# Three regions of SBUF in place of two: where output weights, streams and input weights of the second mixture lie modulo 256 bytes

## The chip, the core and the metric

One core of one Trainium2 chip runs the whole program. The time is device microseconds of that core for one execution. The kernel before takes 1418.29 us (median of three runs, 1417.86 to 1418.48). All data is 32-bit; matrix products run with operands of type fp32r, and to keep precision each product is made of three: a number is split into a high and a low part, and high times high, high times low and low times high are added in PSUM.

## The reference, cut to what matters

```python
def reference(**kw):
    attn = _attn_ref(x, state)               # B, H, S+Ns, D = 8, 8, 544, 64
    x = attn.transpose(0, 2, 1, 3).reshape(4352, 512)
    x = (x @ w_a) * (x @ w_b) @ w_out        # first mixture,  512 -> 1536 -> 512
    h = x @ w_in                             # second mixture, 512 -> 2048
    return (h - tanh(h)) @ w_out2            #                 2048 -> 512
```

Tokens come in nine blocks: blocks 0 to 7 have 512 tokens each (one batch of the attention), block 8 the 256 tokens that the 32 state rows of all batches make.

## The kernel before, in words

**First mixture.** For each block and each of 12 slices f of the hidden width, `AB` (L576) makes two products into PSUM tiles `pab`, multiplies them on VectorE and splits the result into a tile `ph`; `X1` (L602) multiplies `ph` with the slice's output weights `wo` into four accumulators `acc`. In blocks 0 to 7 the weights of `AB` are the small tiles `mx` and the stream (the moving operand) is `hl`, 512 columns wide. In block 8 the weights are `wh` and `wl`, the high and low part of the slice's input weights made in block 1 by `ab_split` (L194), the stream is `x0s`, and every matmul has 256 columns.

**Second mixture.** It runs in 72 slots, eight for each block. A slot of blocks 0 to 7 (`pair_slot`, L755) computes two slices of h by seven half-sized products, `part` (L677): six matmuls of 256 columns each with a piece of the input weights (`wh0`, `wh1` from `wh_load`, L265) as weights and one of the tiles B11 to T4 as stream, into PSUM tiles `px`, `py`, `pz`. The elementwise work of h - tanh(h) (`act_ut` to `g_lo`, L688 to L720) leaves a tile `g`, high and low, and `O` (L722) multiplies `g` as stream, 512 columns, with the output weights `wo2` (`wo_load`, L276) into `acc`. So a slot has 42 matmuls of 256 columns and 24 of 512. The eight slots of block 8 (`plain_slot`, L839) have 24 and 24 matmuls, all of 256 columns.

Every matmul has a weight load of its own, 128 by 128, and the queue of TensorE brings the load of the next matmul beside the stream of the one that runs. The order of work is written out by hand; PE, ACT and DVE each take their instructions in that order, and POOL's queue issues `wo_load` and `wh_load`.

**Where tiles lie.** SBUF tiles come from pools, and the pools are laid one behind the other in the order in which they are opened. Each tile takes a multiple of 256 bytes in a partition, with the exception of the constants (`consts`, 64 bytes, in the pool `step`) and of some at the very end. So all tiles of the pools ahead of `step` start at one residue modulo 256, called 0 here, and all tiles behind it at 64. Slices inside a tile begin at multiples of 256 bytes, so a matmul's operand has the residue of its tile. In the kernel before, the pool `front` has residue 0: the tiles `w` with an even number (`w_tile`, L102) and x6, x7. The pools `wp`, `xp` and `sp` have residue 64: `w` with an odd number, all `v`, x0 to x5, and the slots q, r and m. That puts

- the second mixture's streams B11 to T4 at 0 (`XT`, L632), its input weights `wh0`, `wh1` at 64 (tiles `v`), its output weights `wo2` at 64 (`OPL`, L274) and its stream `g` at 64 (`g_hi`, L713);
- of the first mixture `hl`, `mx`, `ph`, `wo` and `x0s` all at 64; in block 8 the weights `wh` of f = 0 to 7, 10 and 11 at 64, of f = 8 and 9 at 0 (x6, x7), and `wl` at 0, but for f = 0, where it is in q2 at 64.

What follows writes the distance as the stream's residue less the weights'. It is 0 for `O`, `X1` and `AB` of blocks 0 to 7, and -64 for `part`.

Of the kernel before, what the change touches and what calls it, by code (L numbers as in the profile page):

```python
# [29 lines left out]
class Slots:  # L30


    def __init__(self, pool, names):
        self.pool, self.names, self.at = pool, names, {}

    def get(self, shape, dtype, name, among=None):
        among = among or self.names
        key = tuple(among)
        i = self.at.get(key, 0)
        self.at[key] = i + 1  # L40
        return self.pool.tile(shape, dtype, tag=among[i % len(among)], name=name)


@with_exitstack
def fused_kernel(ctx: ExitStack, tc, xT, xn, stp, stq, wA, wB, outT, outS):
# [6 lines left out]
    wp = ctx.enter_context(tc.tile_pool(name="wp", bufs=1))  # L52
    xp = ctx.enter_context(tc.tile_pool(name="xp", bufs=1))
    sp = ctx.enter_context(tc.tile_pool(name="sp", bufs=1))
# [5 lines left out]
    ident = cp.tile([128, 128], F32, tag="ident", name="ident")  # L60
    consts = step.tile([128, 16], F32, tag="consts", name="consts")
    make_identity(nc, ident)
    nc.vector.memset(consts[:, 0:1], PA)
    nc.vector.memset(consts[:, 1:2], -T2)

# [24 lines left out]
    ab = Slots(abp, ["p2", "p3"])  # L90
    big = Slots(sp, [f"q{i}" for i in range(6)])
    small = Slots(sp, [f"r{i}" for i in range(8)])
    mix = Slots(sp, [f"m{i}" for i in range(4)])
    Q, R = big.names, small.names
# [10 lines left out]
    def v_tile(i, shape, dtype, name):  # L105
        return wp.tile(shape, dtype, tag=f"v{i}", name=name)

    def x_tile(i, shape, name, dtype=F32R):
        return (xp if i < 6 else front).tile(shape, dtype, tag=f"x{i}", name=name)

# [162 lines left out]
    WP = {}  # L273
    OPL = [("x", 0)] + [("w", i) for i in range(1, 24, 2)] + [("x", i) for i in (4, 5, 2)]  # L274

    def wo_load(i):  # L276

        f = i // 2 + FP * (i % 2)
        kind, at = OPL[i]
        WB[f] = (w_tile(at, [128, 2, 512], F32R, f"wo2_{f}") if kind == "w"  # L280
                 else x_tile(at, [128, 2, 512], f"wo2_{f}"))
        nc.gpsimd.dma_start(flat(WB[f]), wod[f])
# [293 lines left out]
    def AB(blk, f, bg=None, after=None):  # L576
        n = 512 if blk < NB else 256
        a = None
        for s in range(2):
            pt = ab.get([128, 512], F32, "pab")  # L580
            if blk < NB:
                m = MM[blk, f]
                for G in range(2):
                    product(pt, (m(0, G, s), m(1, G, s)), HL[blk][G], slice(0, n), G == 0, G == 1)
            else:
                for k in range(KT):
                    product(pt, [w[:, s, k, :] for w in WH[f]], X0S[k], slice(0, n), k == 0, k == KT - 1)
            if s == 0:
                a = small.get([128, 512], F32, "ac", AC) if blk < NB else big.get([128, 512], F32, "ac", RAW)
                nc.scalar.copy(a[:, :n], pt[:, :n])  # L590
        if bg:
            bg()
        at_v = nc.vector.tensor_tensor(a[:, :n], a[:, :n], pt[:, :n], ALU.mult)  # L593
        ph = big.get([128, 2, 512], F32R, "ph", PHS)
        at_s = nc.scalar.copy(ph[:, 0, :n], a[:, :n])
        nc.vector.tensor_tensor(ph[:, 1, :n], a[:, :n], ph[:, 0, :n].bitcast(F32), ALU.subtract)
        PH[blk, f] = ph
        if after:
            with tc.issue_after(at_v.ins), tc.issue_after(at_s.ins):
                after()  # L600
# [30 lines left out]
    slots = [(blk, j) for blk in border for j in range(FP)]  # L631
    XT = [[("w", 2 * i) for i in range(7)], [("w", 2 * i) for i in range(7, 12)] + [("x", 6), ("x", 7)]]  # L632

# [3 lines left out]
    def xr_load(blk, parts=(0, 1)):  # L637
        n = 512 if blk < NB else 256
        for i in parts:
            t = x_tile(1, [128, 2, 512], "x1s", F32) if i else big.get([128, 2, 512], F32, "x1r", XIN)  # L640
            for m in range(2):
                nc.sync.dma_start(t[:, m, :n], x1d[blk][2 * i + m])
            RAWX.setdefault(blk, []).append(t)
        XB[blk] = {}
# [53 lines left out]
    def act_k(s, g):  # L698
        u, t, y, k = EW[s, g]
        nc.scalar.activation(k, u, AF.Relu, bias=consts[:, 1:2], scale=1.0)  # L700

# [11 lines left out]
    def g_hi(s, g):  # L713
        GG[s, g] = big.get([128, 2, 512], F32R, "g", Q[2:3] + mix.names[0:2] + Q[0:2])
        nc.scalar.copy(GG[s, g][:, 0, : width(s)], EW[s, g][2])  # L715
# [273 lines left out]
    for f in range(FA):  # L989
        stages = {4: (0,), 5: (1, 2), 6: (3, 4), 7: (5, 6)}.get(f, ())  # L990
        AB(NB, f, after=lambda: [x_stage(0, i) for i in stages])
        if f == 0:
            wo_load(0)
        if f in (3, 7):
# [4 lines left out]
        if f in (9, 10):  # L999
            next(slot)  # L1000
        if f:
            wo_load(f)
        if f in (1, 3):
            xr_load(0, (f // 2,))
    xr_load(1)
    wh_load(2, slots[2][1])
    for i in range(FA + 1, FB):
        wo_load(i)

    last = len(slots) - 1  # L1010
    for s, (blk, j) in enumerate(slots):
# [4 lines left out]
        if blk < NB:  # L1016
            for i, _ in enumerate(pair_slot(s)):
                if s == 1 and i == 0:
                    X1(NB, FA - 1)
                    wo_load(FA)  # L1020
        else:
# [56 lines left out]
```

## Time and profile before

| what | value |
|---|---|
| median of three runs | 1418.29 us |
| the profiled execution | 1418.56 us |
| its span, first to last instruction | 1416.8 us |
| TensorE busy | 1393.3 us, 98% of the span |
| weight loads busy (they overlap the matmuls) | 1187.5 us |
| VectorE busy | 1124.3 us |
| ScalarE busy | 899.1 us |
| granted clock of TensorE | full in all 40 slices |

The page comes from one execution. A matmul's own duration is longer than the step from one matmul to the next, since they are pipelined: the duration of a group along the chain of waits, divided by its matmuls, is the step. The span has three parts: attention and the start of the first mixture up to about 140 us, the first mixture up to 710 us (its block 8 from 648 us), the second mixture behind that, with block 8 from 1360 us.

### The profile page before, as it was taken

How to read it: one execution, taken by the hardware profiler on the slowest of the kernel's cores; microseconds unless marked ns; L12 is line 12 of the kernel's file. 1: busy time of each engine (PE TensorE's matmuls, PEld its weight loads, DVE VectorE, ACT ScalarE, POOL GpSimd, SP SyncE). 2: the span in 40 equal slices, each digit the busy share in tenths (PEclk: the TensorE clock that was granted, in tenths of full speed). 3: DMA queues.
4: the chain of work that ended last, by engine and by line, in shares of the span. 5: the costliest groups of instructions: out<-in, count | busy, mean ns of one | idle time of the engine just before them, and what ended most of it. 6: DMA issues, size and time to landing. Idle time of an engine off the chain costs nothing.

```text
span 1416.8 us, 23918 instructions
## 1 busy us (share of the span) xinstructions
PE 1393.3 (98%) x8928; PEld 1187.5 (84%) x8928; DVE 1124.3 (79%) x1972; ACT 899.1 (63%) x1740; POOL 207.4 (15%) x390
## 2 busy tenths in 40 slices
PE   6999999999999999999999999999999999999998
PEld 3666767888888878889989999999998999999998
DVE  7986656887544879772498999989899898998887
ACT  5765445565444556552477777777777877778675
POOL 0000002333111333321211110111101111011110
PEclk9999999999999999999999999999999999999999
DMA  9614348685546686855876667566665756667544
GB/s 376 259 56 138 128 136 249 212 270 176 160 127 178 178 264 225 251 174 173 259 241 207 202 191 231 179 209 196 208 213 180 230 175 213 207 191 217 164 149 128
DMA packets 103780, 280.49 MB, mean 198 GB/s; under 512 B 15216, under 2 KB 44400, under 8 KB 93936
## 3 DMA queue, kind: packets, MB, share of 16 engines
q0 software_dynamic: 41472, 178.28, 40.8%
q1 hardware_dynamic: 62192, 100.68, 21.9%
q8 instruction: 70, 1.15, 0.3%
q14 instruction: 46, 0.38, 0.1%
HBM read 216.53 MB, written 62.39 MB: 197 GB/s over the span
## 4 chain that ended last, share of the span: by engine, by line
PE 66%; DVE 22%; ACT 8%; issue 3%; DMA 1%; DVEq 0%; SPq 0%; ACTq 0%
PE acc L458 30%; PE pab L458 20%; PE px L680 6%; DVE u L705 3%; DVE y L704 3%; DVE y L709 3%; DVE t L710 3%; PE pz L680 3%; PE mq L546 2%; DVE y L711 2%; ACT g L715 2%; ACT u L691 2%; ACT y L696 2%; PE ph L823 2%; DVE g L720 2%
## 5 line engine op out<-in xcount | busy, mean ns | idle before, releaser
L458 PE MATMUL acc<-g,wo 128*128 128x512 f32 (+1 forms) x1728 | 425.3, 378 | 0.1
L458 PEld LDWEIGHTS acc<-g,wo 128*128 128x128 f32 x1728 | 289.8, 188 | 36.0 <-DVE g L720 0.3
L458 PE MATMUL acc<-ph,wo 128*128 128x512 f32 (+1 forms) x1296 | 305.7, 381 | 0.0
L458 PE MATMUL pab<-hl,mx 128*128 128x512 f32 x1152 | 291.2, 397 | 0.3 <-ACT ac L590 0.2
L458 PEld LDWEIGHTS acc<-ph,wo 128*128 128x128 f32 x1296 | 230.3, 188 | 50.5 <-issue 6.6
L458 PEld LDWEIGHTS pab<-hl,mx 128*128 128x128 f32 x1152 | 209.8, 188 | 52.7 <-issue 4.2
L593 DVE TENSOR_TENSOR ac<-ac,pab 128x512 f32<-128x512 f32 (+1 forms) x108 | 70.6, 654 | 126.0 <-PE pab L458 124.2
L269 POOL DMA_DIRECT2D wh<-whd x144 | 77.6, 539 | 632.9 <-PE pz L680 584.0
L715 ACT CAST g<-y 128x512 fp32r<-128x512 f32 (+1 forms) x144 | 86.2, 598 | 98.6 <-DVE y L711 97.3
L568 POOL DMA_DIRECT2D ml<-md x144 | 75.6, 527 | 408.8 <-DVE mx L574 235.5
L680 PEld LDWEIGHTS px<-T,wh 128*128 128x128 f32 x768 | 105.5, 189 | 13.3 <-ACT snap L782 0.9
L704 DVE SCALAR_TENSOR_TENSOR y<-y,u 128x512 f32<-128x512 f32 (+1 forms) x144 | 94.8, 658 | 27.4 <-ACT y L696 27.2
L590 ACT COPY ac<-pab 128x512 f32<-128x512 f32 (+1 forms) x108 | 60.5, 560 | 83.3 <-PE pab L458 83.0
L680 PE MATMUL px<-T,wh 128*128 128x256 f32 x768 | 111.6, 281 | 0.1
L680 PE MATMUL pz<-T,wh 128*128 128x256 f32 x768 | 111.3, 281 | 0.0
L680 PE MATMUL px<-B,wh 128*128 128x256 f32 x768 | 111.3, 281 | 0.0
L680 PEld LDWEIGHTS px<-B,wh 128*128 128x128 f32 x768 | 104.1, 189 | 5.0 <-ACT snap L791 0.2
L680 PEld LDWEIGHTS pz<-T,wh 128*128 128x128 f32 x768 | 104.1, 189 | 5.0 <-DVE h L794 0.2
L711 DVE COPY_PREDICATED y<-k,t 128x512 f32<-128x512 int32 (+1 forms) x144 | 104.3, 725 | 2.8
L705 DVE SCALAR_TENSOR_TENSOR u<-t,u 128x512 f32<-128x512 f32 (+1 forms) x144 | 94.4, 655 | 9.3 <-ACT k L700 1.0
L720 DVE TENSOR_TENSOR g<-y,g 128x512 fp32r<-128x512 f32 (+1 forms) x144 | 94.4, 656 | 8.2 <-ACT g L715 8.2
L700 ACT ACTIVATE k<-u,consts 128x512 f32<-128x512 f32 (+1 forms) x144 | 99.7, 692 | 0.0
(161 smaller groups left out, 2062.6 us busy)
## 6 DMA issues: line engine op xcount, KB each, us to landing
wh<-whd POOLq DMA_DIRECT2D x64, 1024.0 KB, 5.3
wh<-whd POOLq DMA_DIRECT2D x72, 768.0 KB, 4.7
ml<-md POOLq DMA_DIRECT2D x144, 128.0 KB, 2.9
raw<-in_wB SPq DMA_DIRECT2D x32, 512.0 KB, 4.4
whd<-hlb POOLq DMA_DIRECT2D x64, 256.0 KB, 3.1
rawab<-in_wA SPq DMA_DIRECT2D x12, 1024.0 KB, 9.7
md<-mst SPq DMA_DIRECT2D x48, 256.0 KB, 2.6
x1d<-ev SPq DMA_DIRECT2D x32, 256.0 KB, 3.1
```

Source lines behind the costliest of these rows:

```text
L269: nc.gpsimd.dma_start(t.rearrange("p a h c -> p a (h c)"), whd[j][:, a:b])
L458: nc.tensor.matmul(dst[:, cols], w[a], x[:, c, cols], start=first and i == 0, stop=last and i == 2)
L568: nc.gpsimd.dma_start(t[64 * G : 64 * G + 64, :], src[G, b])
L590: nc.scalar.copy(a[:, :n], pt[:, :n])
L593: at_v = nc.vector.tensor_tensor(a[:, :n], a[:, :n], pt[:, :n], ALU.mult)
L680: nc.tensor.matmul(dst, WP[s, piece][:, a, block(k)], XB[slots[s][0]][x][:, c, k, :], start=first and k == 0 and i == 0, stop=last and k = ...
L700: nc.scalar.activation(k, u, AF.Relu, bias=consts[:, 1:2], scale=1.0)
L704: nc.vector.scalar_tensor_tensor(y, y, PK, u, ALU.add, ALU.mult)
L705: nc.vector.scalar_tensor_tensor(u, t, C3, u, ALU.mult, ALU.mult)
L711: nc.vector.copy_predicated(y, k.bitcast(I32), t)
L715: nc.scalar.copy(GG[s, g][:, 0, : width(s)], EW[s, g][2])
L720: nc.vector.tensor_tensor(gt[:, 1, :n], EW.pop((s, g))[2], gt[:, 0, :n].bitcast(F32), ALU.subtract)
```

## The change

A second pool of 64 bytes (`rise`, with the tile `const2`) stands behind `wp`, so there are three regions: `cp` and `front` at residue 0, `wp` at 64, and the new pool `vp` with `sp` at 128. Tiles move as follows.

- The second mixture's output weights `wo2` go to residue 0: q2 (now in `front`), the even `w` from 0 to 20, x6, x7, x4, x5 (x4 and x5 now in `front`).
- All streams go to 64: B11 to T4 to x0 to x3 and the odd `w` from 1 to 19; `g` to m0, m1, q0, q1 and w21; `hl`, `x0s` and `ph` of blocks 0 to 7 stay at 64, `ph` of block 8 goes to q4 and q5, now at 0.
- The input weights `wh0`, `wh1` (tiles `v`, now in `vp`) go to 128, and with them `wh` of f = 0 to 7 in the first mixture's block 8, while `wh` of f = 10 and 11 and `wl` of f = 0 go to 0. The elementwise tiles r, m2, m3 and q3 go to 128 too; the raw tiles q4, q5 to 0.
- `wo_load(f)` is issued right behind `AB` of block 8, ahead of `X1`, since its tile is now the `wl` that `AB` has just read; `wo_load` of 11 to 15 stands behind `wh_load(2)`; none is left in slot 1. `ac` of block 8 comes from r3 and r4, and half of the raw x1 (`x1s`) lands in w22.

No matmul, elementwise instruction or byte of DMA is added or removed.

```diff
-    def __init__(self, pool, names):
+    def __init__(self, pool, names, homes={}):
...
+        tag = among[i % len(among)]
+        return self.homes.get(tag, self.pool).tile(shape, dtype, tag=tag, name=name)
...
     wp = ctx.enter_context(tc.tile_pool(name="wp", bufs=1))
-    xp = ctx.enter_context(tc.tile_pool(name="xp", bufs=1))
+    rise = ctx.enter_context(tc.tile_pool(name="rise", bufs=1))
+    vp = ctx.enter_context(tc.tile_pool(name="vp", bufs=1))
     sp = ctx.enter_context(tc.tile_pool(name="sp", bufs=1))
...
+    const2 = rise.tile([128, 16], F32, tag="const2", name="const2")
...
-    nc.vector.memset(consts[:, 1:2], -T2)
+    nc.vector.memset(const2[:, 0:1], -T2)
...
-    big = Slots(sp, [f"q{i}" for i in range(6)])
+    big = Slots(sp, [f"q{i}" for i in range(6)], {**{n: front for n in ("q2", "q4", "q5")}, **{n: wp for n in ("q0", "q1", "m0", "m1", "w21")}})
...
-    mix = Slots(sp, [f"m{i}" for i in range(4)])
+    mix = Slots(sp, [f"m{i}" for i in range(4)], {"m0": wp, "m1": wp})
...
     def v_tile(i, shape, dtype, name):
-        return wp.tile(shape, dtype, tag=f"v{i}", name=name)
+        return vp.tile(shape, dtype, tag=f"v{i}", name=name)
...
-        return (xp if i < 6 else front).tile(shape, dtype, tag=f"x{i}", name=name)
+        return (wp if i < 4 else front).tile(shape, dtype, tag=f"x{i}", name=name)
...
-    OPL = [("x", 0)] + [("w", i) for i in range(1, 24, 2)] + [("x", i) for i in (4, 5, 2)]
+    OPL = [None] + [("w", i) for i in range(0, 22, 2)] + [("x", i) for i in (6, 7, 4, 5)]
...
-        ph = big.get([128, 2, 512], F32R, "ph", PHS)
+        ph = big.get([128, 2, 512], F32R, "ph", PHS if blk < NB else RAW)
...
-    XT = [[("w", 2 * i) for i in range(7)], [("w", 2 * i) for i in range(7, 12)] + [("x", 6), ("x", 7)]]
+    XT = [[("x", 2 * b), ("x", 2 * b + 1)] + [("w", 10 * b + 2 * i + 1) for i in range(5)] for b in range(2)]
...
-            t = x_tile(1, [128, 2, 512], "x1s", F32) if i else big.get([128, 2, 512], F32, "x1r", XIN)
+            t = w_tile(22, [128, 2, 512], F32, "x1s") if i else big.get([128, 2, 512], F32, "x1r", XIN)
...
-        GG[s, g] = big.get([128, 2, 512], F32R, "g", Q[2:3] + mix.names[0:2] + Q[0:2])
+        GG[s, g] = big.get([128, 2, 512], F32R, "g", MX + PHS + ["w21"])
...
         AB(NB, f, after=lambda: [x_stage(0, i) for i in stages])
-        if f == 0:
-            wo_load(0)
+        wo_load(f)
...
-        if f:
-            wo_load(f)
...
-    for i in range(FA + 1, FB):
+    for i in range(FA, FB):
         wo_load(i)
...
-                    wo_load(FA)
```

## Rows read from the trace of the kernel before

**Rows 1.** The page's parts 1, 2 and 5: busy time and share; granted clock; weight loads.

```profile
span 1416.8 us, 23918 instructions
...
PE 1393.3 (98%) x8928; PEld 1187.5 (84%) x8928; DVE 1124.3 (79%) x1972; ACT 899.1 (63%) x1740; POOL 207.4 (15%) x390
...
PEclk9999999999999999999999999999999999999999
...
L458 PEld LDWEIGHTS acc<-g,wo 128*128 128x128 f32 x1728 | 289.8, 188 | 36.0 <-DVE g L720 0.3
```

**Rows 2.** Busy time by stage in the second mixture, sum of six stretches of 100 us.

```profile
core 0: us, PE busy (x) PEld busy (x) DVE busy (x) ACT busy (x) POOL busy (x), PEclk, DMA share, GB/s
...
sum 600.00, PE 599.94 PEld 542.27 DVE 548.13 ACT 452.33 POOL 61.96; mean PE 99.99 PEld 90.38 DVE 91.35 ACT 75.39 POOL 10.33
```

**Rows 3.** Chain of waits, second mixture at 1097 us: start, duration, engine, line, count.

```profile
1097.06 0.68 PE acc L458 x3
1097.74 0.71 PE pz L680 x6
1098.45 1.36 PE acc L458 x6
```

**Rows 4.** Groups by shape, PE: count, busy time, mean ns of one, idle time.

```profile
L458 PE MATMUL acc<-g,wo 128*128 128x512 f32 x1536 | 400.1, 389 | 0.0
...
L680 PE MATMUL px<-T,wh 128*128 128x256 f32 x768 | 111.6, 281 | 0.1
```

**Rows 5.** Chain of waits, first mixture's block 8 and the change to the second.

```profile
645.41 2.72 PE acc L458 x12
648.13 2.87 PE pab L458 x24
...
653.75 2.83 PE pab L458 x24
656.58 1.44 PE acc L458 x12
...
683.61 2.72 PE pab L458 x24
...
690.50 0.71 PE py L680 x6
...
694.04 0.68 PE pz L680 x6
...
710.39 0.70 PE acc L458 x3
```

**Rows 6.** Groups by line in 414.24 to 414.26 us, PE alone.

```profile
L458 PE MATMUL acc<-ph,wo 128*128 128x512 f32 x2 | 0.6, 388 | 0.0
```

**Rows 7.** Timeline around these two matmuls: start, duration, engine, line, operation.

```profile
413.79 0.84 PE L458 MATMUL acc<-ph,wo 128*128 128x512 f32 x3
...
414.02 0.19 PEld L458 LDWEIGHTS acc<-ph,wo 128*128 128x128 f32 x1
414.56 0.21 PEld L406 LDWEIGHTS pr<-xnt,E2T 128*32 128x32 f32 x12 [0.35 <-issue]
```

**Rows 8.** Chain of waits, second mixture's block 8.

```profile
1372.16 1.41 PE ph L823 x12
...
1375.01 1.38 PE ph L823 x12
1376.39 1.42 PE acc L458 x12
```

**Rows 9.** Groups by shape, ACT and DVE: operations between tiles of different residues.

```profile
L715 ACT CAST g<-y 128x512 fp32r<-128x512 f32 x128 | 79.7, 622 | 95.7 <-DVE y L711 95.2
...
L649 ACT CAST B<-x1s 128x512 fp32r<-128x512 f32 x17 | 10.5, 624 | 0.0
```

**Rows 10.** Waits in 720 to 1340 us: total, times, longest.

```profile
DVE h L807 <- PE pz L680: 17.3, 33, 0.6
```

More of the change, by code (lines that the diff above doesn't have):

```diff
@@ L30 @@
 class Slots:
-    def __init__(self, pool, names):
-        self.pool, self.names, self.at = pool, names, {}
+    def __init__(self, pool, names, homes={}):
+        self.pool, self.names, self.homes, self.at = pool, names, homes, {}
     def get(self, shape, dtype, name, among=None):
@@ L40, in get @@
         self.at[key] = i + 1
-        return self.pool.tile(shape, dtype, tag=among[i % len(among)], name=name)
+        tag = among[i % len(among)]
+        return self.homes.get(tag, self.pool).tile(shape, dtype, tag=tag, name=name)
 @with_exitstack
@@ L273, in fused_kernel @@
     WP = {}
-    OPL = [("x", 0)] + [("w", i) for i in range(1, 24, 2)] + [("x", i) for i in (4, 5, 2)]
+    OPL = [None] + [("w", i) for i in range(0, 22, 2)] + [("x", i) for i in (6, 7, 4, 5)]
     def wo_load(i):
         f = i // 2 + FP * (i % 2)
-        kind, at = OPL[i]
-        WB[f] = (w_tile(at, [128, 2, 512], F32R, f"wo2_{f}") if kind == "w"
-                 else x_tile(at, [128, 2, 512], f"wo2_{f}"))
+        if i == 0:
+            WB[f] = big.get([128, 2, 512], F32R, "wo2_0", LO0)
+        else:
+            kind, at = OPL[i]
+            WB[f] = (w_tile(at, [128, 2, 512], F32R, f"wo2_{f}") if kind == "w"
+                     else x_tile(at, [128, 2, 512], f"wo2_{f}"))
         nc.gpsimd.dma_start(flat(WB[f]), wod[f])
@@ L588, in AB @@
             if s == 0:
-                a = small.get([128, 512], F32, "ac", AC) if blk < NB else big.get([128, 512], F32, "ac", RAW)
+                a = small.get([128, 512], F32, "ac", AC)
                 nc.scalar.copy(a[:, :n], pt[:, :n])
@@ L699, in act_k @@
         u, t, y, k = EW[s, g]
-        nc.scalar.activation(k, u, AF.Relu, bias=consts[:, 1:2], scale=1.0)
+        nc.scalar.activation(k, u, AF.Relu, bias=const2[:, 0:1], scale=1.0)
     def dve_yu(s, g):
```

## The prediction

> **What bounds the kernel now.** I read the page's busy times and clock first: TensorE is busy in 98% of the span and its clock is full in every slice [rows 1], so the time can change only through what one matmul costs or through a stall. The stages say where: in six stretches of the second mixture PE is busy 599.94 of 600 us, DVE 91%, ACT 75% [rows 2]. There the chain of waits gives the step from matmul to matmul, a group's duration by its count: 0.68 us for three of 512 columns is 227 ns, 0.71 us for six of 256 columns is 118 ns [rows 3]. A slot is 42 × 0.1178 + 24 × 0.2267 = 10.39 us. The change alters no matmul, so all hangs on whether these steps depend on the distance (stream's residue less the weights').
>
> **Where the trace shows that dependence.** Block 8 of the first mixture holds every case side by side, with equal shapes [rows 5]. For f = 0 the stream and all weights are at 64: 24 matmuls take 2.87 us, 120 ns each (the first is short, as it follows 512 columns). For f = 1 to 7, `wh` at 64 and `wl` at 0, 2.83 us, 118 ns. For f = 8 and 9 all weights are at 0 and the stream at 64, a distance of +64: 2.72 us, 113.3 ns. `X1` with 256 columns at distance 0 takes 1.44 us for 12, 120 ns. At distance -64 (`part`) 0.71 us for six is the rule, 118 ns, but some groups take 0.68 us, 113.3 ns: -64 has two states. So for 256 columns: distance 0 costs 120 ns, +64 113.3, -64 mostly 117.8.
>
> Here a rule speaks against the whole change. The Trainium skill, "TensorE: Matmul & The Clock Gate", Part 2, Step-by-step, says that TensorE has two independent read ports, and that loading the next weights takes no bandwidth from the running stream; by it no distance could matter and the sum below would be nothing. The 2.87 against 2.72 us [rows 5] contradict it, at least where a stream is as short as the load.
>
> **512 columns are the decisive case**, since 1536 of them [rows 4] are what goes from distance 0 to +64. Three rows say that they have nothing to win. First, 12 of them at distance 0 take 2.72 us, exactly what 24 of 256 columns take at +64 [rows 5]: the same 0.443 ns per column as in the state that no load disturbs. Second, a matmul of 512 columns beside which nothing is loaded lasts 388 ns: the last of three before 414.6 us starts two steps behind 413.79, and the next load begins at 414.56, when its stream has gone through [rows 6, 7]. With a load beside it, at distance 0, the mean is 389 ns [rows 4]. Third, a load is on record for 188 ns [rows 1], less than the step of 227 and more than that of 118: beside 512 columns it has room to be late, beside 256 it has none. Thus a distance costs where the load is the longer of the two, and `O` in blocks 0 to 7 gains at most 1 ns × 1536 = 1.5 us, which I count as 0.3.
>
> **The change part by part.** (1) `O` in blocks 0 to 7, 0 to +64: -0.3 us (0 to -1.5). Were +64 worse for 512 columns, the nearest row is `acc` x3 in 0.70 us behind a stall [rows 5], 6.7 ns dearer: that is a rival below.
>
> (2) `part`, 2688 matmuls, some 448 groups of six: streams from 0 to 64, weights from 64 to 128, distance -64 as before. Every group enters behind 512-column matmuls whose load has ended early, or behind another group, as now; so I take 0.71 us again, no change. The bounds: 0.68 us, the other state, is -0.03 × 448, or with 117.8 - 113.3 = 4.5 ns × some 2600 not yet in it, -11.7 us; 0.72 us, the price of distance 0, is 2.2 ns × 2600 = +5.7 us. The load of `part`'s first weights beside `O`'s last stream goes from 0 to -64, and that of `O`'s first weights beside `part`'s last stream from -64 to +64: about as many of each, so nothing in sum, 1 us either way.
>
> (3) `O` in block 8, 192 matmuls, 0 to +64: 16 groups of 12, now 1.42 us [rows 8], then 12 × 113.3 = 1.36: -1.0 us. `plain` there is at -64 before and after; behind a group at distance 0 it takes 1.38 us, behind 512 columns 1.41 [rows 8]. Behind +64 I take 1.41, as in block 8 of the first mixture a group behind f = 9 took 0.71 for six [rows 5]: 13 × 0.03 = +0.4 us (0 to +0.5).
>
> (4) First mixture, block 8. f = 10 and 11 go to +64 throughout, 2.83 to 2.72: -0.2 us. f = 0 to 7 get two loads at -64 and one at +64 for each three, between 2.72 and 2.83; with 117.8, 117.8 and 113.3 it is 2.79: -0.4 us (-0.9 to 0). `X1`, 12 groups, 0 to -64: 1.44 to 1.41, -0.4 us (-1.0 to 0). Blocks 0 to 7 keep distance 0 but for six slices of block 1 (`mx` in x4, x5) and half of block 0, at 512 columns: nothing, by the argument above.
>
> (5) ACT and DVE. Their tiles go to other residues. A cast from 64 to 64 takes 622 ns and one from 64 to 0 624 ns [rows 9]: nothing. In the steady slots DVE waits for PE on L807, 17.3 us in 33 waits [rows 10], and it has 9% idle [rows 2], so a slot that is 0.2 us shorter still finds DVE early.
>
> (6) Loads. `wo_load` waits for `AB` of the same f in place of `X1` of the one before; both are waits of POOL's queue alone, and the new one ends one group of `X1` earlier. `wh_load(2)` stands ahead of `wo_load` 11 to 15 on POOL's queue, and has to wait for slot 0's last use of its tile; only these five loads are queued behind it. The first of them is used in slot 5, some 50 us later by the slot's length above. Its cover is that distance; without it, one landing of some us would show. Nothing. `ac` in r3, r4 and `x1s` in w22 have the same number of buffers as before: nothing.
>
> Sum: -0.3 + 0 - 1.0 + 0.4 - 0.2 - 0.4 - 0.4 = -1.9, say **-2 us** (-4 to 0). The profiled execution took 1418.56 us, its span 1416.8 and 1.8 around it; it lies 0.3 above the median. On the median: 1418.3 - 2.0 = **1416.3 us**.
>
> **Rivals.** (a) *`part` falls into its quick state.* Groups of 0.68 us exist at -64 [rows 5], and the load that precedes a group, now at -64 beside 512 columns, may shift the phase. Against it: nearly all groups that enter behind 512 columns are at 0.71 [rows 3]. -11.7 - 1.9 gives 1404.7 us. (b) *512 columns slow down at +64.* The row of 0.70 us for three [rows 5] shows that a load can stretch a 512-column stream. Place: `O`; price 6.7 ns × 1536 = 10.3 us, less 1.6 for the rest of the sum: 1427.0. It decides the sign once the price per matmul is over 1.2 ns. Against it: 256 columns at +64 run undisturbed for 48 matmuls. (c) *`part` becomes as dear as distance 0*, 120 ns: +5.7 - 1.9 gives 1422.1. (d) *Nothing moves*, since the residue of the streams isn't what the rows of block 8 differ in (they also differ in f): 1418.3. This is also what the skill's rule on the two ports gives. (e) *512 columns do carry a price at distance 0*, 6.7 ns as 256 columns do (120 less 113.3): -6.7 × 1536 = -10.3, in all 1406.4. The same page, Back-to-back issue gap, gives N/2.4 + 2.5 ns for an isolated matmul, 215.7 at 512 columns, which would make even 11 ns of the 227 a cost of the load, by estimate some 17 us in all; the matmul without a load, 388 against 389 ns [rows 4, 6], speaks against both.
>
> **How the numbers follow.** Chances: forecast 0.58, (a) 0.17, (b) 0.08, (c) 0.07, (d) 0.06, (e) 0.04. What a measurement tells from no change is 0.2%, 2.8 us. Of the forecast's own range (1414.3 to 1418.3) about a quarter, 0.14, is beyond that on the faster side, so faster 0.14 + 0.17 + 0.04 = 0.35; same 0.44 + 0.06 = 0.50; slower 0.15. Faster and same hold most of the chance: the likeliest case's own range is 1414 to 1418.5; to reach 8 in 10 it is taken down to (a) and (e), whose price has some us of play: 1404 to 1420, which leaves out (b) and (c), 0.15.
>
> **What will show it.** In the chain of waits after: `acc` x6 at 1.36 us in the steady slots (1.32 would be (e), 1.40 (b)); `px` x6 at 0.71 (0.68 is (a), 0.72 (c)); in block 8 `acc` x12 at 1.36 and `ph` x12 at 1.41; in the first mixture's block 8 `pab` x24 at 2.72 for f = 8 to 11 and 2.72 to 2.83 below that (2.83 throughout would be (d)). The means by shape say the same: 389 ns for `acc` of 512 columns, 281 for `px`. PE waiting for `wo` in the second mixture, or DVE without its wait on L807, would make (5) and (6) wrong.

## The result: 1427.84 us against 1418.29, and the profile after

The changed kernel takes 1427.84 us (median; 1427.65 to 1428.35), 1.0069 times the time before, 95% interval 1.0053 to 1.0085: 0.7% slower. One more execution, at a granted clock of 0.56, took 2307.32 us and is not in this range. Its profiled execution took 1427.84 us with a span of 1425.7. The forecast was 1416.3, range 1404 to 1420; what came is rival (b), 512 columns that slow down at +64, priced at 1427.0 and given 0.08. The `matmul` lines L458, L680 and L823 of before are L464, L686 and L829 here.

The page after, span and TensorE, answers to [rows 1]: still 98% busy, 9.7 us more busy time, and the clock is full in all slices as before.

```profile
span 1425.7 us, 23924 instructions
...
PE 1403.0 (98%) x8928; PEld 1190.3 (83%) x8928; DVE 1126.6 (79%) x1972; ACT 902.2 (63%) x1740; POOL 207.5 (15%) x390
```

The groups by shape on PE after (count, busy us, mean ns of one, idle) answer to [rows 4]. The 512-column `acc` went from 389 to 397 ns, the 256-column `px` only from 281 to 282:

```profile
L464 PE MATMUL acc<-g,wo 128*128 128x512 f32 x1536 | 409.9, 397 | 0.0
...
L686 PE MATMUL px<-T,wh 128*128 128x256 f32 x768 | 111.8, 282 | 0.0
```

The chain of waits after, same part of the second mixture as [rows 3] (start, duration, engine, line, count): `acc` x6 at 1.40 us is the sign that the prediction named for (b); `px` x6 stays at 0.71.

```profile
1098.46 0.70 PE acc L464 x3
...
1099.87 1.40 PE acc L464 x6
```

`py` comes once in a slot, so from one `py` in the chain to the next is the length of a slot. Two rows of before, then two of after: 10.38 us became 10.58. From the first `py` of the second mixture to the last, the trace of after is 10.4 us longer.

```profile
1110.21 0.71 PE py L680 x6
...
1120.59 0.71 PE py L680 x6
```

```profile
872.04 0.71 PE py L686 x6
...
882.62 0.71 PE py L686 x6
```

From start to start in the trace, the 1536 matmuls of `O` go from 227.3 to 233.6 ns, +9.7 us; the 2688 of `part` from 117.9 to 118.3, +1.2 us; the 256-column work of the two blocks 8 gives 1.9 us back. Together that is +9.0, of 9.3 between the two profiled executions.

The chain of waits after in the first mixture's block 8, beside [rows 5]: f = 0 to 7 now 2.74 us and `X1` 1.42, f = 8 at 2.83 where it was 2.72, f = 9 still 2.72, f = 10 at 2.83.

```profile
648.02 2.74 PE pab L464 x24
...
682.58 2.83 PE pab L464 x24
...
686.78 2.72 PE pab L464 x24
...
693.70 2.83 PE pab L464 x24
```

The same view in the second mixture's block 8, beside [rows 8]: from 1386 us on, `acc` and `ph` at 1.36 us for 12.

```profile
1388.87 1.36 PE acc L464 x12
1390.23 1.36 PE ph L829 x12
```

The waits after in 720 to 1340 us (total us, times, longest), beside [rows 10]: DVE still waits for PE.

```profile
DVE h L813 <- PE pz L686: 22.3, 32, 0.8
```

### The profile page after: what moved, and what is told of

The parts are those of the page before. It is cut to its first block, busy times and chain, and to the rows that moved or that the text cites. A ratio compares the mean times of both kernels' runs of the same rounds, so it can differ in the third digit from the quotient of the medians.

```text
span 1425.7 us, 23924 instructions
## 1 busy us (share of the span) xinstructions
PE 1403.0 (98%) x8928; PEld 1190.3 (83%) x8928; DVE 1126.6 (79%) x1972; ACT 902.2 (63%) x1740; POOL 207.5 (15%) x390
## 4 chain that ended last, share of the span: by engine, by line
PE 92%; DVE 5%; ACT 1%; issue 1%; DMA 1%; SPq 0%; DVEq 0%; ACTq 0%
PE acc L464 44%; PE pab L464 19%; PE px L686 13%; PE pz L686 6%; PE py L686 3%; PE mq L552 2%; PE ph L829 1%; PE sc L337 1%; DMA md<-mst 1%; PE pt L349 0%; PE mp L503 0%; PE pr L412 0%; DVE wa L133 0%; DVE wa L134 0%; DVE mst L559 0%
## 5 line engine op out<-in xcount | busy, mean ns | idle before, releaser
L464 PE MATMUL acc<-g,wo 128*128 128x512 f32 (+1 forms) x1728 | 434.3, 384 | 0.1
L464 PEld LDWEIGHTS acc<-g,wo 128*128 128x128 f32 x1728 | 291.4, 189 | 40.3 <-DVE g L726 0.3
L464 PE MATMUL acc<-ph,wo 128*128 128x512 f32 (+1 forms) x1296 | 305.8, 381 | 0.0
L464 PE MATMUL pab<-hl,mx 128*128 128x512 f32 x1152 | 291.4, 397 | 0.3 <-ACT ac L596 0.2
L464 PEld LDWEIGHTS acc<-ph,wo 128*128 128x128 f32 x1296 | 229.9, 188 | 51.0 <-issue 6.6
L464 PEld LDWEIGHTS pab<-hl,mx 128*128 128x128 f32 x1152 | 209.8, 188 | 52.8 <-issue 4.2
L686 PEld LDWEIGHTS px<-T,wh 128*128 128x128 f32 x768 | 107.9, 188 | 12.1 <-ACT snap L788 0.8
L686 PE MATMUL px<-B,wh 128*128 128x256 f32 x768 | 112.1, 281 | 0.0
L686 PE MATMUL px<-T,wh 128*128 128x256 f32 x768 | 111.8, 282 | 0.0
L686 PE MATMUL pz<-T,wh 128*128 128x256 f32 x768 | 111.7, 281 | 0.0
L686 PEld LDWEIGHTS px<-B,wh 128*128 128x128 f32 x768 | 104.1, 189 | 6.2 <-ACT snap L797 0.4
L686 PEld LDWEIGHTS pz<-T,wh 128*128 128x128 f32 x768 | 104.0, 189 | 6.1 <-DVE h L800 0.3
L706 ACT ACTIVATE k<-u,const 128x512 f32<-128x512 f32 (+1 forms) x144 | 99.7, 693 | 0.0
```

Of the source, the lines that this page charges most:

```text
L464: nc.tensor.matmul(dst[:, cols], w[a], x[:, c, cols], start=first and i == 0, stop=last and i == 2)
L686: nc.tensor.matmul(dst, WP[s, piece][:, a, block(k)], XB[slots[s][0]][x][:, c, k, :], start=first and k == 0 and i == 0, stop=last and k = ...
L706: nc.scalar.activation(k, u, AF.Relu, bias=const2[:, 0:1], scale=1.0)
```

## The experiments

Theory 1: TensorE's own step depends on where stream and weights lie. Theory 2: the step is stretched from outside, by other engines' accesses or by the new order of loads. A placement is four distances: of `O`, of `part`, and of the two loads at the seams, `part`'s first weights beside `O`'s last stream (O→part) and `O`'s first weights beside `part`'s last stream (part→O).

### Bare chains: distance alone

The kernel `map` holds chains of 36 matmuls, with nothing beside them but small copies on ScalarE and a DMA of zeros, and computes none of the reference:

```python
CHAINS = [("L", d) for d in range(0, 256, 16)] + [("H", d) for d in range(0, 256, 16)]
CHAINS += [("M", d) for d in (0, 64, 128, 192)] + [("L", d) for d in (0, 320, 64, 0)]
```

> A kernel that leaves the whole computation out and writes no results: only chains of 36 matmuls, fp32r, each with its own weight load, no other engine busy, at distances (stream's residue less the weights', modulo 256 bytes) of 0, 16, ... 240, with 512 columns (tiles La to Lp) and with 256 (Ha to Hp), four distances with 384 (Ma, Me, Mi, Mm), and 512 at distance 320. Theory 1, the distance alone makes the step of a matmul, in opposite ways for the two widths: 512 columns 227 ns at 0, 233 at 64 and at 320, about 237 at 192; 256 columns 120 ns at 0, 113.3 at 64, 118 at 192. Theory 2, the slower steps come from what ACT, DVE and DMA do beside the matmuls: 227 ns at every distance with 512 columns.

Chain of waits of this kernel; L is 512 columns, H 256, the letter behind it the distance in steps of 16 bytes (a 0, c 32, e 64, g 96):

```profile
41.73 8.26 PE Le L65 x36
...
58.27 8.40 PE Lg L65 x36
...
142.21 4.31 PE Ha L65 x36
...
150.83 4.20 PE Hc L65 x36
...
159.23 4.24 PE He L65 x36
...
260.18 8.17 PE La L65 x36
```

Busy time by stage of the same kernel, 10 to 230 us (stretch, sum, then PE, weight loads, VectorE, ScalarE, GpSimd, clock, DMA share, GB/s): VectorE and GpSimd do nothing, and ScalarE's 140 copies are the same behind every chain.

```profile
10.00:230.00 220.00, 220.00 (x1260) 194.89 (x1259) 0.00 (x0) 22.25 (x140) 0.00 (x0) 1.00 0.08 31
```

Per matmul 512 columns cost 226.7 ns at distance 0 (8.17 / 36 = 227), 228.9 at +64 and 233.3 at most others; 256 columns cost 120.0 at 0 and 116.7 to 117.8 at 32 and 64. At 320 the chain takes 8.24 us, as at 64. Most distances were taken once. So the step depends on the distance with VectorE idle and nothing changed but the weights' address, and 512 columns have their best place at 0 (and at 16), where they stood before. Theory 1's own figures missed: 233 ns were expected at +64 and 113.3 for 256 columns there. +64 costs 2.2 ns here and 6.3 in the kernel, so distance isn't the whole. The Trainium skill, "TensorE: Matmul & The Clock Gate", Part 2, Step-by-step, has loading the next weights take no read bandwidth from the running matmul. The 8.17 against 8.40 us, equal but for where the weights lie, disagree.

### The placement in the whole kernel

Six kernels differ from after or before in the size of the constants alone, which shifts everything behind them. 

> The changed kernel with one thing undone: the constants ahead of the second region take 256 bytes in place of 64, so streams and output weights are at distance 0 again, while the input weights stay 64 bytes behind the streams, and loads, order and tiles stay as changed. Theory 1 (the distance of O makes the loss): 1536 steps fall from 233.6 to 227 ns, 10 us, and the matmuls beside a load of part's first weights, now at 237, to 237 still: 1417 to 1420 us. Theory 2 (another part of the change, such as the order of the loads or the elementwise tiles that lie 64 bytes from the streams as they do after): 1427 to 1428 us, steps of 233.

> As the one before, but the input weights 192 bytes behind the streams, so part is at distance +64 and O at 0: the distance at which each width was quickest. Theory 1: px steps from 118 to 113.3 ns, 2688 x 4.5 = 12 us less than with part at -64; O's last matmul ahead of part has its neighbour's load at +64, 233 in place of 237: 1405 to 1409 us. If part's step hangs on the 512-column matmuls around it and not on the distance: 1417 to 1420 us.

> The changed kernel with 128 bytes of constants ahead of the second region: O at distance +128, part at -64 still. Theory 1 says that what O costs follows the distance as in the bare chains: if 128 is as free there as 0, 1417 to 1420 us, if it costs 6 ns as 64 does, 1427 us. Theory 2: 1427 us whatever the bare chains show.

> The kernel before with 192 bytes of constants ahead of the second region in place of 64, and nothing else: the streams of part get to +64 from the input weights in place of -64; O stays at 0, and so does the load of part's weights beside O's last stream; the load of O's weights beside part's last stream goes from -64 to +64. Theory 1 revised: O stays at 227 ns, and px takes 113.3 to 117.8: 1406 to 1418 us. Theory 2: 1418 us, 118 and 227 ns.

> The kernel before with 256 bytes of constants: every distance is 0, at the seams too. Theory 1 revised: O at 227 ns, px at 120 ns, +2.2 x 2688 = 6 us: 1424 us. Theory 2: 1418 us.

> The changed kernel with 256 bytes in both pools of constants: every distance 0, as in b_c256, but with the tiles, loads and order of the change. Theory 1 revised: the same time as b_c256 within 2 us, about 1424 us, acc at 227 ns. Theory 2, if the order of the loads or the tiles cost something: above b_c256 by what they cost, 5 us or more, with acc still at 232 ns.

```diff
# o0_pm64 (from after); o128_pm64 has 32 here, o0_p0 has 64 in both
-    consts = step.tile([128, 16], F32, tag="consts", name="consts")
+    consts = step.tile([128, 64], F32, tag="consts", name="consts")
# o0_pp64 has besides
-    const2 = rise.tile([128, 16], F32, tag="const2", name="const2")
+    const2 = rise.tile([128, 48], F32, tag="const2", name="const2")
# b_c192 (from before); b_c256 has 64
-    consts = step.tile([128, 16], F32, tag="consts", name="consts")
+    consts = step.tile([128, 48], F32, tag="consts", name="consts")
```

The slot in this table is one slot of each kernel near 1100 us, from `py` to `py`; those of o0_pp64 vary from 10.42 to 10.49.

| kernel | O, part, O→part, part→O | slot, us | time, us | ratio to before |
|---|---|---|---|---|
| before | 0, -64, 0, -64 | 10.39 | 1418.29 | |
| after | +64, -64, -64, +64 | 10.58 | 1427.84 | 1.0069 [1.0053, 1.0085] |
| o0_pm64 | 0, -64, -64, 0 | 10.47 | 1424.36 | 1.0044 [1.0029, 1.0059] |
| o0_pp64 | 0, +64, +64, 0 | 10.46 | 1423.68 | 1.0037 [1.0023, 1.0052] |
| o128_pm64 | +128, -64, -64, +128 | 10.54 | 1426.61 | one run |
| b_c192 | 0, +64, 0, +64 | 10.50 | 1425.43 | 1.0053 [1.0036, 1.0070] |
| b_c256 | 0, 0, 0, 0 | 10.56 | 1429.27 | 1.0080 [1.0065, 1.0095] |
| o0_p0 | 0, 0, 0, 0 | 10.55 | 1430.41 | 1.0087 [1.0072, 1.0102] |

The last two have the same distances, one on the old kernel and one on the changed one with its new order of loads and tiles; they differ by 1.1 us. So the rest of the change costs about nothing, and theory 2's loads are out. But the sums of theory 1 missed in five of the six runs: o0_pm64 came 4 us above its range, o0_pp64 15, b_c192 7, and b_c256 and o0_p0 lie 5 and 6 above their 1424; all distances at 0 gave `O` steps of 231.5 ns, not 227. `O` back at 0 with `part` as before (o0_pm64) should have given 1417 to 1420; its `acc` has steps of 231.8 ns, not 227. In the slots it differs from before in the seams alone, and is 0.08 us longer. The seams count, and the prediction had netted them to nothing.

### Bare slots: all 64 placements

The kernel `slotmap` runs two slots of 42 and 24 matmuls in the kernel's order for each of 64 placements, with small copies on ScalarE between them and no work on VectorE or GpSimd, and computes none of the reference.

```python
ORDER = "p p a a p p a p a a p a p a a".split()   # a: 3 of 512 columns, p: 6 of 256
```

> The computation is left out and no results are written: only the matmuls of a slot of blocks 0 to 7 in their order (42 of 256 columns, 24 of 512, groups of 6 and 3), two slots for each of the 64 placements of output weights, streams of part and input weights at 0, 64, 128, 192 bytes from the stream g (letters a to d in this order behind o or p in the tiles' names); no other engine works beside it. Theory 1, revised (the sequence of distances decides, with the loads at the seams between groups, where the last stream of one kind runs beside the load of the next kind): before's placement, oada and pada, gives 10.39 us a slot; the changed one, odab and pdab, 10.54; o0_pm64's, oaab, 10.49; o128_pm64's, ocab, 10.52. Theory 2 (ACT, DVE, DMA or the order of loads make the difference in the kernels): all four within 0.03 us of each other.

Chain of waits of this kernel, first group of two placements (tile names end in the placement: `ada` is before, `dab` after); to the first group of the next placement it is two slots:

```profile
262.67 1.41 PE pada L77 x12
...
283.44 1.42 PE padb L77 x12
...
1041.10 1.37 PE pdab L77 x12
...
1061.74 1.42 PE pdac L77 x12
```

A slot takes 10.385 us for `ada` (10.39 in the kernel); the second slot takes 10.46 for the placement of o0_pm64, 10.42 for o0_pp64, 10.54 for o128_pm64, 10.51 for b_c192, 10.55 for distance 0 throughout: within 0.04 us of the table with VectorE and GpSimd idle. The stream `g` lies at 0 in all bare slots and at 0, 64, 128 or 192 in these kernels, so the distances count and not the residue itself. The lengths of the second slot run from 10.25 to 10.64 over the 64, and that of before is among the six shortest. One stands out. The changed kernel's own placement, expected at 10.54, takes 10.32 bare and 10.58 in the kernel: by this map it should have been 4 us faster than before.

### One placement, two lengths

> Bare slots again (24 matmuls of 512 columns and 42 of 256 in the kernel's order, TensorE alone), three placements (that of the changed kernel, dab; all four distances at +64, dad; that of the kernel before, ada), each three slots long after ten different beginnings: a slot of another placement, cut off after 16, 15, ... 7 of its 16 groups. The slot map gave dab 10.32 us a slot, but the changed kernel settles at 10.58 in its own slots. Theory 1 (the step goes by the distances and by the state that the work before left behind): dab settles at two or more values, 10.32 after some beginnings and 10.58 after others, while ada always comes to 10.39 to 10.40. Theory 3 (the distances alone decide in bare slots, and something that only the whole kernel has, other engines or waits, costs the changed kernel 0.26 us a slot): dab gives 10.32 after every beginning. dad shows by the same means whether its 10.25 can be relied on.

The kernel `slotmap2`: three placements, each with three slots behind ten beginnings.

```python
BEFORE = "ada aaa aab aba cab dad dda bbc ddd bdd".split()
order = ORDER[: 16 - n] if s == 0 else ORDER      # the beginning, cut off
```

Chain of waits, first group of consecutive slots of `dab`: first behind a slot of `ada`, then behind one of `aab`.

```profile
42.33 1.42 PE pdab L78 x12
...
52.90 1.42 PE pdab L78 x12
```

```profile
115.22 1.37 PE pdab L78 x12
...
125.54 1.37 PE pdab L78 x12
```

10.57 and 10.32 us for the same tiles in the same order. `dab` settled at 10.58 behind three of the ten beginnings and at 10.32 behind seven; `dad`, all four distances at +64, at 10.25, 10.44 or 10.51; `ada`, the placement of before, at 10.39 behind all ten. So a placement has one or more lengths, and what ran just before chooses.

Expected of `dad` in the whole kernel:

> The changed kernel with 192 bytes in place of 64 ahead of the second mixture's input weights: they come to the residue of the output weights, and each of the four loads lies 64 bytes below the stream beside it (O +64, part +64, both seams +64; dad in the slot map). Theory 1 with the slot map's figure: 10.25 us a slot against 10.39 in the kernel before, 64 slots, 8 to 9 us faster than before: 1409 to 1411; if it has a second state as dab seems to have, 10.5 to 10.6 a slot and 1424 to 1430. Theory 2 (the order of loads and the other tiles of the change cost the time): 1426 to 1430.

```diff
-    const2 = rise.tile([128, 16], F32, tag="const2", name="const2")
+    const2 = rise.tile([128, 48], F32, tag="const2", name="const2")
```

It took 1425.2 us, ratio 1.0052 [1.0035, 1.0068], and stood at 10.507 us a slot: a long state again.

### What moves TensorE from one state to the other

> TensorE alone, bare slots of the placements dab (the changed kernel) and dad (all four at +64). Each first gets one slot of another placement and one of its own, so that it stands in its long state (10.58 us a slot for dab, 10.51 for dad) or in its short one (10.32 and 10.25); then one or two extra matmuls are put in, of 512 or 256 columns, with weights at one of four residues; then two more slots. Theory 1 (the length of a slot is a state of TensorE's own that the work before leaves behind, and nothing takes it away): some of the extra matmuls move a slot from the long to the short state for good, 0.26 us a slot less at the cost of 0.11 to 0.47 us once, and the others leave it. If the states go by the beginning alone and not by phase: none of them changes a slot that comes after.

```python
KICKS = [(512, 3, 1), (512, 0, 1), (512, 1, 1), (512, 2, 1), (256, 3, 1), (256, 0, 1),
         (256, 1, 1), (256, 2, 1), (512, 3, 2), (256, 3, 2)]   # columns, residue of weights / 64, count
```

None of the ten took `dab` out of 10.58, and five threw it out of 10.32. `dad` went from 10.51 to 10.25 with any single matmul of 512 columns.

> The changed kernel's placement (dab), bare, standing in its long state of 10.58 us a slot, from which none of the ten insertions of the kick map took it. 29 longer or other insertions of 1 to 9 matmuls (256, 384 or 512 columns, weights at four residues). Theory 1: some of them move it to 10.32 for good, since seven of ten beginnings led there. If the long state of dab catches every disturbance: all 29 give 10.58 again, and the 10.32 depends on more than what stands just before.

18 of the 29 took `dab` from 10.58 to 10.32, among them one matmul of 384 columns with weights at any of the four residues. Chain of waits around the one with weights 192 bytes above the stream's residue: twelve of 256 columns take 1.42 us before it and 1.37 behind it, a slot of 10.32 between the last two shown.

```profile
363.48 1.42 PE pdab L83 x12
...
374.16 1.37 PE pdab L83 x12
...
384.48 1.37 PE pdab L83 x12
```

### The whole kernel in the other state

> The kernel with all four distances at +64 stood at 10.507 us a slot from its 13th slot on, the long state of its bare slots. Here one more matmul of 512 columns is put ahead of the first output matmul of blocks 1 to 7 (its sum is overwritten by the one behind it, so nothing else changes), with weights 64 bytes above the stream, as the kick map has it. Theory 1 (the state is TensorE's own, and a matmul out of step moves it): 10.25 us a slot from block 1 on, 56 slots x 0.254 = 14.2 us less, 7 x 0.23 = 1.6 more: 1425.2 - 12.6 = 1412 to 1414, faster than the kernel before though it does more work. Theory 3 (in the whole kernel other engines or waits hold the slot at 10.507): 1426 to 1428, the extra matmuls on top.

```diff
+        if j == 0 and g == 0 and m == 0 and 0 < blk < NB:
+            nc.tensor.matmul(acc[0], WB[0][:, 0, 32:160], GG[s, 0][:, 0, 0:512], start=True, stop=False, skip_group_check=True)
         product(acc[m], pair(WB[j + FP * g], block(m)), GG[s, g], slice(0, n), j == 0 and g == 0,
```

It took 1425.35 us, ratio 1.0054 [1.0038, 1.0071]: no gain. Chain of waits around the extra matmul of block 1 (L735):

```profile
794.30 0.23 PE acc L735
...
795.23 0.68 PE px L686 x6
...
803.44 0.77 PE px L686 x6
```

The short step is there at once, 0.68 us, and ends nine microseconds later at a group that took 0.77. The timeline at that place (start, duration, engine, line, operation, idle time and what ended it):

```profile
802.28 0.62 ACT L721 CAST g<-y 128x512 fp32r<-128x512 f32 x1 [1.01 <-DVE y L717]
802.81 0.36 ACT L790 COPY snap<-px 128x256 f32<-128x256 f32 x1
...
803.23 0.77 PEld L686 LDWEIGHTS px<-T,wh 128*128 128x128 f32 x6 [0.23 <-ACT snap L790]
```

`px` may not be added to before ScalarE has copied it, and that copy stood behind a cast that waits for VectorE. At the long step nobody notices; at the short step PE arrives 60 ns early, waits, and is in the long state.

With this the trace of after reads differently. The changed kernel too began its second mixture with `py` at 0.69 us and a slot of 10.32 (745.47 to 755.79), and lost it at the same copy, which came 15 to 20 ns too late. Timeline, then chain of waits, of after at 770 us:

```profile
770.01 0.62 ACT L721 CAST g<-y 128x512 fp32r<-128x512 f32 x1 [1.01 <-DVE y L717]
...
770.54 0.36 ACT L788 COPY snap<-px 128x256 f32<-128x256 f32 x1
...
770.96 0.77 PEld L686 LDWEIGHTS px<-T,wh 128*128 128x128 f32 x6 [0.18 <-ACT snap L788]
```

```profile
769.14 0.69 PE px L686 x6
...
771.21 0.72 PE px L686 x6
...
773.32 0.71 PE px L686 x6
```

From 776.8 us on every slot is 10.58 us. Not every late copy ends the short state: ten microseconds earlier, at 760.6, the same copy held PE up for 0.18 us, and the short step went on. The runs that follow try to take that wait away.

> In the kernel with the extra matmuls the slot behind each of them came to the short step (px at 113 ns), until within one or two slots the second px<-T of a slot came 60 ns late, behind ScalarE's copy snap<-px, which had stood behind the cast g<-y; from there the slot was back at 10.507. Here that copy is put ahead of the cast (with the VectorE work on the same g moved behind it), nothing else changes. Theory 1 with this cause of the fall-back: the short state holds, 10.25 us a slot, 56 slots: 1410 to 1414. If another wait comes next, or if the state falls back without one: 1422 to 1426.

```diff
-            g_hi(s - 1, 0)
...
         part(x_, s, 3, "T2", False, True)
         nc.scalar.copy(sn[:, 1], x_)
+        if s:
+            g_hi(s - 1, 0)
+            g_lo(s - 1, 0)
+            dve_rest(s - 1, 1)
```

1424.57 us, ratio 1.0043 [1.0027, 1.0060]. It told nothing of the wait: ScalarE's queue came out in the same order as before, cast first, and the second `px<-T` was late again by 55 to 80 ns in eleven slots.

> The changed kernel itself, all tiles where the change puts them, with the same copy ahead of the cast and three more matmuls of 512 columns once, at the first output matmul of block 1, with weights at the stream's residue: in bare slots of this placement these three led from 10.58 to 10.32 us a slot. Theory 1 (the changed kernel's loss belongs to the state, not to the distances as such): 56 slots x 0.26 = 14.6 us less and 0.7 more: 1413 to 1416, less than the kernel before. If the distances alone cost the time: 1427 to 1429; if the state is reached but a wait throws it out: 1422 to 1428, with slots of 10.32 in the trace between.

The same edit, from after, with these three matmuls at block 1:

```diff
+        if j == 0 and g == 0 and m == 0 and blk == 1:
+            for c in (0, 1, 0):
+                nc.tensor.matmul(acc[0], WB[0][:, 0, 16:144], GG[s, 0][:, c, 0:512], start=True, stop=False, skip_group_check=True)
```

1427.62 us, ratio 1.0067 [1.0052, 1.0082]. With the wait still there, block 0 ran one slot at 10.32 us and two at 10.35, in which the second `px<-T` was 25 to 33 ns late and the state held. From the second slot behind the three matmuls on all were at 10.58. The copy was late in the slot of the insertion too, by 31 ns; the run doesn't tell which of the two ended the short state.

> In the run before, the copy snap<-px written earlier in the code stood behind the cast in ScalarE's queue all the same (the instructions are ordered by a planner), and the 60 ns wait of the second px<-T went on. Here an explicit edge puts the cast behind the copy. Theory 1 with that wait as the cause of the fall-back: no px<-T at 180 ns any more and the short state holds, 10.25 us a slot in most of blocks 1 to 7: 1410 to 1414. If another wait comes next at this pace (the cast is now 0.3 us later): slots of 10.25 to 10.5, 1415 to 1425. If the state falls back with no wait: 1424 to 1426.

> The changed kernel with the same edge and one extra matmul of 384 columns at the first output matmul of block 2. In the run before, the changed kernel's tiles ran four slots of block 0 at 10.34 to 10.37 us and fell to 10.58 at the very insertion that was to help. Theory 1 (the loss belongs to the state): slots of 10.32 us, either in blocks 0 and 1 or from block 2 on, and 0.26 us less for each of them than in the changed kernel: 1413 to 1424. If the distances alone cost the time: 10.58 throughout, 1427 to 1429.

```diff
# both: the edge that puts the cast behind the copy
+        taken = nc.scalar.copy(sn[:, 1], x_)
+        if s:
+            with tc.issue_after(taken.ins):
+                g_hi(s - 1, 0)
# after_kick_first: the extra matmul
+        if j == 0 and g == 0 and m == 0 and blk == 2:
+            nc.tensor.matmul(acc[0][:, 0:384], WB[0][:, 0, 16:144], GG[s, 0][:, 0, 0:384], start=True, stop=False, skip_group_check=True)
```

after_kick_first has every tile where the change puts it. Its chain of waits, behind the extra matmul (L735, at 876.87 us) and 150 us later:

```profile
891.49 0.69 PE py L686 x6
...
892.87 1.37 PE acc L464 x6
...
901.81 0.69 PE py L686 x6
```

```profile
1036.29 0.71 PE py L686 x6
...
1037.71 1.40 PE acc L464 x6
...
1046.87 0.71 PE py L686 x6
```

Slots of 10.32 and of 10.58 us in one execution, `acc` x6 at 1.37 and at 1.40. It ran 17 slots at 10.32: four of block 0, where after has one before its stall, and 13 behind the extra matmul. From the first `py` to the last it is 4.3 us shorter than after. It took 1423.52 us (1422.86 to 1423.88), 4.3 less than after, ratio 1.0040 [1.0025, 1.0054]. In the short state the steps of `O` are 229.2 ns, the price of +64 in the bare chains, and in the long one 233.8, at the same distances. What the changed kernel loses goes with the state, not with the distance as such.

o64_p64_kick_first took 1421.80 us, ratio 1.0028 [1.0018, 1.0038]. Its chain of waits behind the extra matmul of block 1:

```profile
797.80 0.68 PE py L686 x6
...
808.05 0.68 PE py L686 x6
```

10.25 us a slot, and the second `px<-T` is late behind none of the seven insertions: three slots at 10.25 follow four of the insertions, where not one followed any in the two runs before, so that wait did end the state there. Yet in the fourth slot the short state ends, at 10.44 three times in four and else at 10.51. An insertion that finds 10.44 leads to 10.51 and one that finds 10.51 leads to 10.25, in all seven blocks: each state has its successor. For this the full gain (1410 to 1414) did not come. No version beats the kernel before.

What ends the short state in these two runs is a wait too short for the chain of waits to list. In the slots behind the extra matmul, VectorE's instruction that makes the low half of `g` starts 10.35 us after that of the slot before, while PE's slots are 10.25. Timeline of VectorE in o64_p64_kick_first, third and fourth slot:

```profile
823.52 0.68 DVE L726 TENSOR_TENSOR g<-y,g 128x512 fp32r<-128x512 f32 x1
...
833.87 0.68 DVE L726 TENSOR_TENSOR g<-y,g 128x512 fp32r<-128x512 f32 x1
```

The weight load that waits for this `g` comes 10.32 us later in the fourth slot than in the third, where the slots so far had 10.25; it is some 60 ns late:

```profile
824.29 0.19 PEld L464 LDWEIGHTS acc<-g,wo 128*128 128x128 f32 x1
...
834.61 0.19 PEld L464 LDWEIGHTS acc<-g,wo 128*128 128x128 f32 x1
```

PE's step turns long at this matmul. The traces of the two runs have seven ends of a short stretch, and all look alike: from slot to slot `g` ends later behind the slot's `py`, by some 100 ns at 10.25 us a slot and by 10 to 40 at 10.32, until it ends 6.13 to 6.17 us behind it. In four of the seven PE first slips at the load for `g`, 15 to 57 ns late; in three it slips by 3 to 9 ns at the first `px<-T`, whose load follows a copy of ScalarE (L777), and the load for `g` is over 70 ns late in the same slot. The two slots of 10.35 in after_kick_early go at the same pace.

So VectorE and ScalarE together take about 10.35 us for a slot in these kernels, and the 10.39 of before lies close above it. By an estimate from these slots, a faster TensorE could gain 64 × 0.04 = 2.6 us on the kernel before and no more. This is read from traces; no run makes VectorE's work shorter to test it.

## Why the prediction was wrong, point by point

**What bounds the kernel** held: PE 98% busy, no stall, all in the step.

**(1) is the step that failed**: "a distance costs where the load is the longer of the two, and `O` in blocks 0 to 7 gains at most 1 ns", counted as -0.3 us. It measured +6.3 ns × 1536 = +9.7 us, close to rival (b)'s 6.7. For 512 columns the three rows behind it were all taken at distance 0, and they showed rightly that nothing is to be won *from there*: 226.7 ns is the floor of the bare chains too. They say nothing of +64. From "no cost at 0" I concluded "no cost at any distance" because the load is shorter than the stream; the bare chains have 233.3 ns at most distances and 228.9 at +64, with the same load and the same stream. And what 256 columns do says nothing of 512: their order is reversed, 120.0 at 0, where 512 are best.

**The method below (1) failed as well**: the sum gave each matmul a price by its own distance and netted the seams. o0_pm64 keeps both own distances of before and its slots cost 64 × 0.08 = 5 us more by their seams. And one placement has more than one price, so no sum over distances could give the sign: at 10.32 us a slot the second mixture would have been 4 us faster than before (64 × 0.07), beyond the forecast; it began there, met a late copy and settled at 10.58, and by the estimate above VectorE's pace would not have let it stay. Of "-64 has two states" the prediction had the right observation, for 256 columns, and used it as a rival for `part` alone.

**(2)** held in size: `px` x6 at 0.71 us; 118.3 for 117.9 ns, +1.2 us, inside its bounds of -11.7 and +5.7.

**(3)** held for `acc`, 1.36 us for 12 as said, behind the first groups. `ph` came to 1.36, not 1.41: -0.9 us in all, where -0.6 was counted.

**(4)** f = 0 to 7: 2.74 us, inside 2.72 to 2.83, a little better than the 2.79 taken. `X1` 1.42, taken 1.41. f = 10 and 11 stayed at 2.83 and did not come to 2.72, though they lie as f = 8 and 9 do, and f = 8 itself, whose place did not change, went from 2.72 to 2.83: a second place where the distance did not fix the step. (3) and (4) together: -1.9 us, -1.6 counted.

**(5)** held at the pace that came: DVE still waits for PE (22.3 us in 32 waits, 17.3 before). Its reason did not: that a slot 0.2 us shorter still finds DVE early was read from 9% idle time, and at slots of 10.25 and 10.32 us VectorE fell behind from slot to slot. This bears on rival (a) too, whose 11.7 us would have needed slots near 10.2.

**(6)** held: PE never waits for `wo`, and o0_p0 against b_c256 puts the rest of the change at 1.1 us or less.

**Rivals.** (b) came true in sign, place and size, with a mechanism that is only half right: not a load that stretches a 512-column stream at +64 as such (bare: 2.2 ns), but a state that the slots fall into. That its price, taken from one group behind a stall, came so near is in part luck. (d), nothing moves, falls with the bare chains. (a), `part` in its quick state, exists: the short state of after_kick_first has `py` at 0.69 us.

## What to carry to other kernels

When PE is the bound and its step is all that can move, a price for an address belongs to the whole repeating sequence of matmuls and loads, seams included: measure the sequence bare, behind several different beginnings, before believing a sum over single distances. A placement that returns to one length from every beginning is worth more than one with a shorter best case. If a kernel is in the long one, look for waits of some tens of nanoseconds that only the short one meets, a late weight load among them, and ask first what pace the next engine can keep: its idle share does not tell.

## What the hardware showed that I had not expected

- With VectorE and GpSimd idle, the step depends on the distance between stream and weights modulo 256 bytes: 226.7 to 233-234 ns at 512 columns, 116.7 to 120.0 at 256; distance 0 is the best place for 512 columns and the worst for 256.
- The same 66 matmuls on the same tiles take 10.32 or 10.58 us (10.25, 10.44 or 10.51 at +64 throughout), by what ran before them, and keep that length until something disturbs them: one extra matmul of 384 columns, or a weight load that comes 15 to 80 ns late, though not every late one does it.
- The placement of before has one length, 10.39 us, behind all ten beginnings.
- VectorE, 91% busy before, falls behind TensorE at 10.25 and at 10.32 us a slot: with ScalarE it takes about 10.35.
- Open: what in the chip the state is, and why one late load ends it and another doesn't.
